# First MLP in six tiles of 512 tokens instead of eight of 384, with attention ending in the fourth tile

## The chip, the cores and the metric

The kernel runs on one core of a Trainium2 chip. The metric is the device time of one execution in microseconds (us), the median over several runs. Engines are named as in the profile: PE is the matrix engine (TensorE), PEld its weight loads, DVE the vector engine, ACT the scalar engine, POOL GpSimd, SP the engine whose queue issues nearly all DMAs here.

## The reference

Chunked attention feeds a first MLP, and that a second MLP, all in float32:

```python
# attention: q, k, v [4, 8, 768, 64], chunks of 32 queries; each sees 8 memory keys,
# 16 keys to the left, its own 32 and 8 to the right
scores = scale * np.matmul(q_c, k_full.transpose(0, 1, 3, 2))
scores = scores - np.max(scores, axis=-1, keepdims=True)
a = np.exp(scores)
a = a / (np.sum(a, axis=-1, keepdims=True) + 1e-09)
out[:, :, c_start:c_end] = np.matmul(a, v_full)
...
# first MLP: x [3072, 512], w_in [512, 2048], w_out [2048, 512]
h = x @ w_in
g = np.where(h > 0.0, h, alpha * (np.exp(np.minimum(h, 0.0)) - 1.0))
x = (g @ w_out).astype(np.float32)
# second MLP, same sizes
h = x @ w_in
r = np.maximum(h, 0.0)
g = s * (r * r) + b
return (g @ w_out).astype(np.float32)
```

## The kernel before

**Attention** works on 24 units of 128 tokens (four chunks, all heads). A unit goes through three steps: `step_S` (scores into a PSUM tile psS, then the softmax on DVE with its exponential on ACT, into `sm`), `step_P` (the transpose of `sm` into `pt`) and `step_V` (values into psV, then `to_x`). For the first `NU0` units (6) the steps are issued separately and `step_P` transposes on PE (psP, line 251) with a copy by ACT. From unit `NU0` on `step_P` uses 16 DVE stream transposes (line 258), and `step_VS` puts the values of one unit and the scores of the next behind each other on PE (psVS). The results of the first two tiles are split at once into a high and a low fp32r part (`xh`, `xl`); later ones go to DRAM (`x_dram`) and come back with `load_x`.

**First MLP.** Its tokens are cut into eight tiles of 384 (`sizes`), its hidden units into 16 blocks c of 128. A step (t, c) is `h1`: 12 matmuls of 128 x 128 weights against 384 columns into one PSUM bank psH (4 blocks of the contraction, three products each: high x high, high x low, low x high), then on ACT and DVE the activation `g` and its split into gh and gl; and, two steps behind, `out1`: 12 matmuls into four PSUM banks acc, three into each. I call 12 such matmuls a half-step and number the steps 0 to 127. The order of steps is written out: tile 0 with blocks 0 to 5, all of tile 1, the rest of tile 0 (its first part goes by way of `part_dram`), then tiles 2 to 7. So step 6 is (1, 0), step 22 is (0, 6), step 32 is (2, 0).

**Work beside the MLP steps.** `beside` mixes attention into the steps: units 0 to 2 come ahead of step 0, units 3 to 5 beside steps 0 to 5, none in tile 1, units 6 to 8 beside the rest of tile 0, the others evenly over tiles 2 to 4 (up to `TATT`). The weights of the first MLP arrive as int64 bits of doubles; `weights_to` turns them into fp32r pairs with work on ACT and DVE (`to_f32`, `split_w`), up to the end of tile 1. From `TATT` on `prepared` does the like for the second MLP's weights (`prepare`, with sums for a Strassen-like scheme) into `s_dram`, until `NFREE` blocks of the last tile are done. Then the buffers of the first `NFREE` blocks' weights (pool wpa) are given up and `load_blocks` fetches the second MLP's input.

**Second MLP.** Three tiles of 1024 tokens, seven products instead of eight blocks; every matmul there has 512 columns already (psH with `xc` moving, then psL with g2h and g2l moving).

The order within an engine is fixed when the program is built, by a scheduler that follows the order of the code with small shifts; each engine runs its instructions in that order. 16 KB of each partition are kept for descriptors of DMAs that GpSimd issues; the kernel issues none there.

Of the kernel before, what the change touches and what calls it, by code (L numbers as in the profile page):

```python
# [27 lines left out]
NP = H // 2  # L28
NU0 = 6
HF = 6  # L30
TATT = 5
NFREE = 8
MICRO = 8
# [20 lines left out]
def tile_attention_then_two_mlps(ctx, tc, q_in, k_in, v_in, w1, w2, s_in, b_in, out):  # L54
# [27 lines left out]

    sizes = [3] * 8
    assert sum(sizes) == NU
# [213 lines left out]
    def load_x(t):  # L298

        X[t] = xh, xl = x_tiles((t + 1) % 2)  # L300
        nc.sync.dma_start(out=f(xl), in_=x_dram[:, :, starts[t] * U:(starts[t] + sizes[t]) * U])
        nc.scalar.activation(out=xh, in_=f(xl), func=AF.Copy)
        sub(xl, f(xl), xh)
# [60 lines left out]
    def put_out(t, c, n):  # L364
# [6 lines left out]
        if c == NF - 1 or c == HF - 1 and split:  # L371
            for m, acc in enumerate(ACC[t]):
                with tc.high_priority(400):
                    if c == NF - 1 and split:
                        o = PART.pop(m)
                        nc.vector.tensor_tensor(out=o, in0=o, in1=acc[:, :n], op=ALU.add)
                    else:
                        o = big_tile(n, t >= TATT and m > 0 or m == 3 and t >= 2)
                        if m % 2:
                            nc.vector.tensor_copy(o, acc[:, :n])  # L380
                        else:
                            nc.scalar.activation(out=o, in_=acc[:, :n], func=AF.Copy)
                store = nc.scalar if t == NTILE1 - 1 else nc.sync
                store.dma_start(out=y_dram[:, m, t0:t0 + n] if c == NF - 1 else part_dram[:, m, :n], in_=o)
# [184 lines left out]
    def mlp1_step(t, c):  # L569
# [6 lines left out]
        elif t == 0:  # L576
            a0, total, k, ks = ready[1], ready[2] - ready[1], min(c - HF, NF - HF - 4), NF - HF - 3
        elif 1 < t < TATT:
            a0, total, k, ks = ready[2], len(steps) - ready[2], NF * (t - 2) + c, NF * (TATT - 2)

# [4 lines left out]
        elif t == 1:  # L585
            n0 = 8 * HF + 12
            wt = [(w1, max(n0 + (MICRO * NF - n0) * (2 * c + z) // 28, MICRO * (c + z)), 4) for z in (1, 2)]
        if c == 0 and t == TATT:
            actx.close()
# [24 lines left out]
    def prepared(t, n):  # L614

        want = min(NPREP * (2 * NF * (t - TATT) + n) // (2 * NF * (NTILE1 - TATT) - 2 * (NF - NFREE)), NPREP)
        while t >= TATT and p2["n"] < want:
            next(p2["steps"])
            p2["n"] += 1
# [182 lines left out]
```

## Time and profile before

| what | value |
|---|---|
| median of 3 runs | 1097.02 us (1095.85 to 1098.19) |
| the profiled execution: its own time | 1097.48 us |
| its span | 1095.7 us |
| PE busy in the span | 1076.3 us (98%) |
| DVE busy | 783.9 us (72%) |
| ACT busy | 591.9 us (54%) |
| mean granted PE clock | 0.992 of full speed |

Busy time of PE counts a matmul from its start to its modelled end, and matmuls overlap, so 98% does not say that the array works at its peak; the spacing of starts says how fast the stream runs. The span leaves out 1.78 us of the execution's own time.

### The profile page before, as it was taken

Reading aid. Unit: us, or ns where it says so; the run is one execution under the profiler, and the core shown is the slowest. Engines: PE = TensorE matmul, PEld = TensorE weight load, DVE = VectorE, ACT = ScalarE, POOL = GpSimd, SP = SyncE. Lnnn points to the kernel's source line nnn. Section 1 sums busy time; section 2 is a strip of 40 time slices with the busy share of each in tenths; the row PEclk is TensorE's granted clock in tenths of the full one; section 3 lists DMA queues with packets and bytes.
Section 4 is the critical chain, followed back from the end, with each engine's and each line's share of the span. In section 5 each row is a group of like instructions: output and inputs, shape, how many; then the busy total and the mean of one; then the engine's idle time right before and its main releaser. Section 6 shows DMA issues by size and latency. Waiting matters only on the chain.

```text
span 1095.7 us, 20629 instructions
## 1 busy us (share of the span) xinstructions
PE 1076.3 (98%) x8206; PEld 964.4 (88%) x8206; DVE 783.9 (72%) x1299; ACT 591.9 (54%) x939; POOL 0.7 (0%) x6
## 2 busy tenths in 40 slices
PE   7999999999999999999999999999999999999998
PEld 5889999999999999999999987788888788888886
DVE  6899856777777777898884656796266695375844
ACT  4888534344344346887875455644355653355542
POOL 0000000000000000000000000000000000000000
PEclk7999999999999999999999999999999999999999
DMA  8965032442433316888876366777767777776773
GB/s 305 377 223 214 1 109 94 146 144 93 142 117 121 114 40 206 328 329 303 328 289 253 90 192 190 240 211 224 229 192 196 222 207 226 207 193 192 205 190 124
DMA packets 98113, 213.70 MB, mean 195 GB/s; under 512 B 9952, under 2 KB 27360, under 8 KB 95968
## 3 DMA queue, kind: packets, MB, share of 16 engines
q1 hardware_dynamic: 97440, 211.59, 60.3%
q8 instruction: 65, 1.06, 0.4%
q10 hardware_dynamic: 576, 0.79, 0.2%
q14 instruction: 32, 0.26, 0.1%
HBM read 164.89 MB, written 47.45 MB: 194 GB/s over the span
## 4 chain that ended last, share of the span: by engine, by line
PE 87%; DVE 6%; DMA 4%; ACT 3%; issue 1%; SPq 0%; ACTq 0%; DVEq 0%
PE psH L326 14%; PE psH L328 14%; PE psH L327 14%; PE psL L327 7%; PE psL L328 7%; PE acc L326 7%; PE psL L326 7%; PE acc L327 7%; PE acc L328 7%; DVE pt L258 2%; DMA xc<-y_dram 1%; PE psVS L278 1%; DMA xl<-x_dram 1%; PE psVS L219 1%; PE psV L278 1%
## 5 line engine op out<-in xcount | busy, mean ns | idle before, releaser
L326 PE MATMUL psH<-xh,w 128*128 128x384 f32 x512 | 174.9, 342 | 2.4 <-ACT pt L180 1.0
L326 PE MATMUL acc<-gh,w 128*128 128x384 f32 x512 | 172.7, 338 | 1.3 <-DVE big L380 0.8
L328 PE MATMUL psH<-xh,w 128*128 128x384 f32 x512 | 173.0, 338 | 0.0
L327 PE MATMUL psH<-xl,w 128*128 128x384 f32 x512 | 172.6, 337 | 0.2 <-DVE xl L184 0.2
L328 PE MATMUL acc<-gh,w 128*128 128x384 f32 x512 | 171.8, 336 | 0.0
L327 PE MATMUL acc<-gl,w 128*128 128x384 f32 x512 | 171.7, 335 | 0.0
L702 ACT ACTIVATE g2h<-g 128x1024 fp32r<-128x1024 f32 x84 | 88.9, 1058 | 95.6 <-PE psL L328 95.5
L327 PE MATMUL psL<-g2l,ws 128*128 128x512 f32 x336 | 133.0, 396 | 1.4 <-DVE g2l L184 1.4
L184 DVE TENSOR_TENSOR g2l<-g,g2h 128x1024 fp32r<-128x1024 f32 x84 | 102.3, 1222 | 44.3 <-ACT g2h L702 44.0
L328 PE MATMUL psL<-g2h,ws 128*128 128x512 f32 x336 | 132.9, 395 | 0.0
L326 PE MATMUL psL<-g2h,ws 128*128 128x512 f32 x336 | 132.5, 396 | 0.1
L326 PE MATMUL psH<-xc,ws 128*128 128x512 f32 x336 | 131.7, 397 | 0.5 <-ACT p L653 0.5
L327 PE MATMUL psH<-xc,ws 128*128 128x512 f32 x336 | 131.0, 390 | 0.0
L328 PE MATMUL psH<-xc,ws 128*128 128x512 f32 x336 | 131.0, 390 | 0.0
L350 ACT ACTIVATE g<-psH 128x384 f32<-128x384 f32 x128 | 62.5, 488 | 111.9 <-PE psH L328 65.3
L180 ACT ACTIVATE gh<-g 128x384 fp32r<-128x384 f32 x128 | 67.0, 523 | 88.0 <-DVE g L352 86.9
L352 DVE SCALAR_TENSOR_TENSOR g<-g,psH 128x384 f32<-128x384 f32 x128 | 70.4, 550 | 47.8 <-ACT g L351 46.9
L326 PEld LDWEIGHTS psH<-xh,w 128*128 128x128 f32 x512 | 96.7, 189 | 5.1 <-ACT pt L180 1.2
L326 PEld LDWEIGHTS acc<-gh,w 128*128 128x128 f32 x512 | 96.1, 188 | 2.8 <-DVE big L380 1.1
L327 PEld LDWEIGHTS psH<-xl,w 128*128 128x128 f32 x512 | 96.7, 189 | 0.5 <-DVE xl L184 0.4
L328 PEld LDWEIGHTS psH<-xh,w 128*128 128x128 f32 x512 | 96.7, 189 | 0.2
L327 PEld LDWEIGHTS acc<-gl,w 128*128 128x128 f32 x512 | 96.2, 188 | 0.1
(97 smaller groups left out, 1667.9 us busy)
## 6 DMA issues: line engine op xcount, KB each, us to landing
ws<-s_dram SPq DMA_DIRECT2D x336, 256.0 KB, 3.0
raw<-w SPq DMA_DIRECT2D x64, 512.0 KB, 5.5
s_dram<-right SPq DMA_DIRECT2D x16, 1024.0 KB, 4.6
kb<-k SPq DMA_DIRECT2D x24, 512.0 KB, 5.5
v<-v SPq DMA_DIRECT2D x24, 512.0 KB, 4.1
s_dram<-left SPq DMA_DIRECT2D x16, 768.0 KB, 3.6
q<-q SPq DMA_DIRECT2D x24, 256.0 KB, 5.4
out<-r SPq DMA_DIRECT2D x24, 256.0 KB, 3.5
```

Source lines behind the costliest of these rows:

```text
L180: return nc.scalar.activation(out=hi, in_=src, func=AF.Copy)
L184: return nc.vector.tensor_tensor(out=lo, in0=src, in1=f(hi), op=ALU.subtract)
L219: mm = nc.tensor.matmul(ps[o, z, r * NCK:(r + 1) * NCK], q[rows, r * U + c * CH:r * U + (c + 1) * CH], kb[rows, r, c * NCK:(c + 1) * NCK], ...
L258: nc.vector.transpose(out=pt[k * CH:(k + 1) * CH, :, rows], in_=sm[rows, :, z, n0:n0 + CH])
L278: nc.tensor.matmul(ps[r % 2 * D:(r % 2 + 1) * D, z, o:o + CH], v[rows, (r * NC + c) * D:(r * NC + c + 1) * D], pt[rows, r, cs], start=True ...
L326: nc.tensor.matmul(o, sa(a[0]), sb(b[0]), start=first, stop=False, skip_group_check=again)
L327: nc.tensor.matmul(o, sa(a[0]), sb(b[1]), start=False, stop=False, skip_group_check=again)
L328: return nc.tensor.matmul(o, sa(a[1]), sb(b[0]), start=False, stop=last, skip_group_check=again)
L350: nc.scalar.activation(out=g[:, :n], in_=ps[:, :n], func=AF.Relu, scale=-1.0)
L352: nc.vector.scalar_tensor_tensor(out=g[:, :n], in0=g[:, :n], scalar=-1.0, in1=ps[:, :n], op0=ALU.add, op1=ALU.max)
L702: nc.scalar.activation(out=gh, in_=g[:, block], func=AF.Copy)
```

## The change

The first MLP gets six tiles of 512 tokens (four units each). Tile 0 now takes units 0 to 3 ahead of step 0, tile 1 units 4 to 7 beside steps 0 to 5, units 8 to 11 stand beside the rest of tile 0, and units 12 to 23 in tile 2 and the first eight steps of tile 3 (`ATT_END`). Separate attention steps with PE transposes go to eight units (`NU0`), the pool given up early holds ten blocks (`NFREE`), and preparation of the second MLP's weights runs from step (3, 8) to step (5, 10). The descriptor space shrinks from 16 KB to 1 KB to make room for the wider buffers. There are 96 steps now; step 22 is still (0, 6).

```diff
--- before.py
+++ after.py
@@ -26,10 +26,10 @@
 UPB = S // U
 NU = B * UPB
 NP = H // 2
-NU0 = 6
+NU0 = 8
 HF = 6
-TATT = 5
-NFREE = 8
+ATT_END = (3, 8)
+NFREE = 10
 MICRO = 8
 HN, NT2 = 512, 3
 ORDER = (1, 2, 6, 5, 7, 3, 4)
@@ -80,7 +80,7 @@
         n = turn[step, phase[0]] = turn.get((step, phase[0]), -1) + 1
         return names[n % len(names)]
 
-    sizes = [3] * 8
+    sizes = [4] * 6
     assert sum(sizes) == NU
     MAXN = max(sizes) * U
     starts = [sum(sizes[:i]) for i in range(len(sizes))]
@@ -297,7 +297,7 @@
 
     def load_x(t):
 
-        X[t] = xh, xl = x_tiles((t + 1) % 2)
+        xh, xl = X[t] = tuple(x[:, :, :sizes[t] * U] for x in x_tiles((t + 1) % 2))
         nc.sync.dma_start(out=f(xl), in_=x_dram[:, :, starts[t] * U:(starts[t] + sizes[t]) * U])
         nc.scalar.activation(out=xh, in_=f(xl), func=AF.Copy)
         sub(xl, f(xl), xh)
@@ -375,7 +375,7 @@
                         o = PART.pop(m)
                         nc.vector.tensor_tensor(out=o, in0=o, in1=acc[:, :n], op=ALU.add)
                     else:
-                        o = big_tile(n, t >= TATT and m > 0 or m == 3 and t >= 2)
+                        o = big_tile(n, len(op) > 1 and m > 0 or m == 3 and t >= 2)
                         if m % 2:
                             nc.vector.tensor_copy(o, acc[:, :n])
                         else:
@@ -575,8 +575,8 @@
             a0, total, k, ks = ready[0], ready[1] - ready[0], c, HF
         elif t == 0:
             a0, total, k, ks = ready[1], ready[2] - ready[1], min(c - HF, NF - HF - 4), NF - HF - 3
-        elif 1 < t < TATT:
-            a0, total, k, ks = ready[2], len(steps) - ready[2], NF * (t - 2) + c, NF * (TATT - 2)
+        elif t > 1 and (t, c) < ATT_END:
+            a0, total, k, ks = ready[2], len(steps) - ready[2], NF * (t - 2) + c, NF * (ATT_END[0] - 2) + ATT_END[1]
 
         wt = [(w1, 0, 4)] * 2
         if t == 0 and c < HF:
@@ -585,7 +585,7 @@
         elif t == 1:
             n0 = 8 * HF + 12
             wt = [(w1, max(n0 + (MICRO * NF - n0) * (2 * c + z) // 28, MICRO * (c + z)), 4) for z in (1, 2)]
-        if c == 0 and t == TATT:
+        if (t, c) == ATT_END:
             actx.close()
             op.append(mctx.enter_context(tc.tile_pool(name="op2", bufs=2)))
             p2["prep"] = early[1].enter_context(tc.tile_pool(name="prep", bufs=2, side="right", reuse_waits="tile"))
@@ -613,8 +613,9 @@
 
     def prepared(t, n):
 
-        want = min(NPREP * (2 * NF * (t - TATT) + n) // (2 * NF * (NTILE1 - TATT) - 2 * (NF - NFREE)), NPREP)
-        while t >= TATT and p2["n"] < want:
+        begin = 2 * (NF * ATT_END[0] + ATT_END[1])
+        want = min(NPREP * (2 * NF * t + n - begin) // (2 * NF * (NTILE1 - 1) + 2 * NFREE - begin), NPREP)
+        while (t, n) > (ATT_END[0], 2 * ATT_END[1]) and p2["n"] < want:
             next(p2["steps"])
             p2["n"] += 1
 
@@ -782,7 +783,7 @@
     import concourse.bacc as bacc
     from concourse.bass_utils import run_bass_kernel_spmd
 
-    nc = bacc.Bacc("TRN2", target_bir_lowering=False, num_devices=1)
+    nc = bacc.Bacc("TRN2", target_bir_lowering=False, num_devices=1, dynamic_dma_scratch_size=1024)
     q, k, v = pack(q, k, v, mem_k, mem_v)
     arrays = {
         "q": q,
```

How this moves instructions is shown at three places. Names end in buffer numbers where one operation has several.

First, PE around the first step of the first MLP (psP and psV are steps of attention, psS scores, sm_103 and sm_104 the two softmax buffers in turn, w_0 the weights of block 0). Before:

```order
L251 MATMUL psP<-ident,sm_103 128x128 x4
L278 MATMUL psV<-pt,v 64x32 x32
L219 MATMUL psS<-kb,q 32x64 x32
L326 MATMUL psH<-xh,w_0_382 128x384
L327 MATMUL psH<-xl,w_0_382 128x384
```

After, from the same row on:

```order
L251 MATMUL psP<-ident,sm_103 128x128 x4
L278 MATMUL psV<-pt,v 64x32 x32
L219 MATMUL psS<-kb,q 32x64 x32
L251 MATMUL psP<-ident,sm_104 128x128 x4
L278 MATMUL psV<-pt,v 64x32 x32
L219 MATMUL psS<-kb,q 32x64 x32
L326 MATMUL psH<-xh,w_0_433 128x512
L251 MATMUL psP<-ident,sm_103 128x128 x4
L327 MATMUL psH<-xl,w_0_433 128x512
```

One more unit (transposes of sm_104, values, scores) stands ahead of the first psH matmul, and the transposes of the unit behind it come after that first matmul instead of after the whole half-step.

Second, DVE in tile 1, from one activation g to the next (raw, t and w are the conversion of the weights, the number behind the name is the block). Before:

```order
L352 SCALAR_TENSOR_TENSOR g<-g,psH 128x384
L184 TENSOR_TENSOR w_7_1131<-t,w_7_1131 128x512
L138 SCALAR_TENSOR_TENSOR t<-raw_8_977,t 128x512
L184 TENSOR_TENSOR gl<-g,gh 128x384
L135 SCALAR_TENSOR_TENSOR t<-raw_8_1043 128x512
L135 SCALAR_TENSOR_TENSOR t<-raw_9_1081 128x512
L184 TENSOR_TENSOR w_8_1186<-t,w_8_1186 128x512
L138 SCALAR_TENSOR_TENSOR t<-raw_8_1043,t 128x512
L352 SCALAR_TENSOR_TENSOR g<-g,psH 128x384
```

After:

```order
L352 SCALAR_TENSOR_TENSOR g<-g,psH 128x512
L138 SCALAR_TENSOR_TENSOR t<-raw_8_1157,t 128x512
L135 SCALAR_TENSOR_TENSOR t<-raw_8_1223 128x512
L135 SCALAR_TENSOR_TENSOR t<-raw_9_1261 128x512
L380 COPY big<-acc_893 128x512
L184 TENSOR_TENSOR gl<-g,gh 128x512
L184 TENSOR_TENSOR w_8_1366<-t,w_8_1366 128x512
L138 SCALAR_TENSOR_TENSOR t<-raw_8_1223,t 128x512
L138 SCALAR_TENSOR_TENSOR t<-raw_9_1261,t 128x512
L352 SCALAR_TENSOR_TENSOR g<-g,psH 128x512
```

Both pieces run from the activation of step 7, (1, 1), to that of step 8. Six conversions and one gl stand between the two in either; after has a copy of an accumulator (big, acc) besides, which stood ahead of step 7 before, and g and gl have 512 columns.

Third, PE at the last attention unit (one psV, since no scores follow). Before:

```order
L328 MATMUL acc_4655<-gh,w_13_1597 128x384
L326 MATMUL acc_4656<-gh,w_13_1597 128x384
L327 MATMUL acc_4656<-gl,w_13_1597 128x384
L328 MATMUL acc_4656<-gh,w_13_1597 128x384
L278 MATMUL psV<-pt,v 64x32 x32
L326 MATMUL psH<-xh,w_0_382 128x384
L327 MATMUL psH<-xl,w_0_382 128x384
```

After:

```order
L328 MATMUL acc_4270<-gh,w_5_1136 128x512
L326 MATMUL acc_4271<-gh,w_5_1136 128x512
L327 MATMUL acc_4271<-gl,w_5_1136 128x512
L328 MATMUL acc_4271<-gh,w_5_1136 128x512
L278 MATMUL psV<-pt,v 64x32 x32
L326 MATMUL psH<-xh,w_8_1366 128x512
L327 MATMUL psH<-xl,w_8_1366 128x512
```

It stood behind the out1 of block 13 of tile 4, with block 0 of tile 5 next; it now stands behind block 5 and ahead of block 8 of tile 3.

## Rows read from the trace of the kernel before

**Rows 1.** The page's busy times: engine, busy us (share of the span), instructions

```profile
PE 1076.3 (98%) x8206; PEld 964.4 (88%) x8206; DVE 783.9 (72%) x1299; ACT 591.9 (54%) x939; POOL 0.7 (0%) x6
```

**Rows 2.** The page's granted PE clock in 40 slices of 27.4 us, tenths of full speed

```profile
PEclk7999999999999999999999999999999999999999
```

**Rows 3.** Stretches by stage: start:end length, busy us of each engine, PE clock, DMA, GB/s

```profile
0.00:28.30 28.30, 21.46 (x546) 16.67 (x546) 18.02 (x38) 12.22 (x20) 0.70 (x6) 0.78 0.84 308
28.30:76.20 47.90, 43.64 (x586) 38.48 (x578) 45.06 (x93) 41.80 (x81) 0.00 (x0) 0.95 0.77 294
76.20:136.60 60.40, 60.36 (x386) 58.99 (x387) 55.55 (x106) 43.83 (x86) 0.00 (x0) 1.00 0.35 130
136.60:182.90 46.30, 46.21 (x499) 45.34 (x498) 28.79 (x66) 18.60 (x35) 0.00 (x0) 1.00 0.37 116
182.90:416.80 233.90, 231.48 (x3010) 224.82 (x3008) 174.32 (x421) 96.04 (x182) 0.00 (x0) 1.00 0.34 110
416.80:550.30 133.50, 133.50 (x773) 133.50 (x770) 116.15 (x215) 105.90 (x197) 0.00 (x0) 1.00 0.85 307
550.30:621.10 70.80, 70.80 (x409) 70.80 (x408) 48.29 (x79) 42.38 (x78) 0.00 (x0) 1.00 0.57 210
621.10:1095.70 474.60, 468.88 (x2018) 375.79 (x2016) 297.69 (x284) 231.13 (x264) 0.00 (x0) 1.00 0.71 202
```

**Rows 4.** Stretches without attention, PE alone: 384 columns, psL, psH of the second MLP

```profile
470.00:600.00 130.00, 130.00 (x751) 1.00 0.83 305
1015.00:1090.00 75.00, 75.00 (x323) 1.00 0.63 179
807.00:821.50 14.50, 14.50 (x66) 1.00 0.70 195
```

**Rows 5.** Timeline of PE, second MLP, first and last psH of an unbroken run

```profile
806.68 0.39 PE L326 MATMUL psH<-xc,ws 128*128 128x512 f32 x1
...
821.41 0.39 PE L328 MATMUL psH<-xc,ws 128*128 128x512 f32 x1
```

**Rows 6.** Timeline of PE at the start: start us, length, operation [idle before]

```profile
22.79 1.11 PE L251 MATMUL psP<-ident,sm 128*128 128x128 f32 x4
...
24.65 1.72 PE L278 MATMUL psV<-pt,v 64*64 64x32 f32 x56 [0.75 <-ACT pt L180]
...
26.86 0.44 PE L278 MATMUL psV<-pt,v 64*64 64x32 f32 x8 [0.49 <-issue]
...
27.22 1.18 PE L219 MATMUL psS<-kb,q 64*32 64x64 f32 x64
...
28.34 0.69 PE L326 MATMUL psH<-xh,w 128*128 128x384 f32 x1
...
32.09 0.52 PE L328 MATMUL psH<-xh,w 128*128 128x384 f32 x1
...
32.41 0.82 PE L251 MATMUL psP<-ident,sm 128*128 128x128 f32 x4
```

**Rows 7.** Timeline of DVE: softmax end of unit 3, activations g of steps 0 and 6

```profile
29.98 0.68 DVE L237 TENSOR_TENSOR sm<-sm,rs 128x512 f32<-128x512 f32 x1
...
33.73 0.55 DVE L352 SCALAR_TENSOR_TENSOR g<-g,psH 128x384 f32<-128x384 f32 x1 [1.87 <-ACT g L351]
...
75.64 0.55 DVE L352 SCALAR_TENSOR_TENSOR g<-g,psH 128x384 f32<-128x384 f32 x1
```

**Rows 8.** Timeline of PE, last acc and first psH around one psVS step

```profile
239.72 0.34 PE L328 MATMUL acc<-gh,w 128*128 128x384 f32 x1
...
241.84 0.44 PE L326 MATMUL psH<-xh,w 128*128 128x384 f32 x1
```

**Rows 9.** Groups by line, DVE: count, busy us, mean ns, idle before

```profile
L352 DVE SCALAR_TENSOR_TENSOR g<-g,psH 128x384 f32<-128x384 f32 x128 | 70.4, 550 | 47.8 <-ACT g L351 46.9
...
L138 DVE SCALAR_TENSOR_TENSOR t<-raw,t 128x512 int32<-128x512 int32 x64 | 43.8, 686 | 0.4
...
L258 DVE STREAM_TRANSPOSE pt<-sm 32x128 f32<-32x128 f32 x288 | 87.1, 303 | 5.8
```

## Prediction, made before the changed kernel ran

> **What bounds the kernel now.** I read the busy times first: PE is taken for 98% of the span, DVE for 72%, ACT for 54% [rows 1]. That is a mean over unlike stages, so next I cut the span where the order of steps changes [rows 3]; the eight lengths add up to 1095.7 us. The reader should see two kinds of stage. From 76.2 us on PE is busy almost without a gap in every stage (231.48 of 233.9 us in the stretch with most of the attention, all of 133.5 and 70.8 us behind it): there the time is the number of matmuls by the spacing of their starts, plus what attention puts between them. Ahead of 76.2 us it isn't so. PE is busy for 21.46 of the first 28.3 us and its clock is 0.78; from 28.3 to 76.2 us DVE is busy for 45.06 of 47.9 us, so it sets the pace there. The second MLP (621.1 to the end, 474.6 us) has neither new instructions nor another order, and I take it as it is.
>
> The spacing comes from stretches without attention [rows 4]. A window counts every matmul that touches it, so I add one matmul's length to the window: (130 + 0.34)/751 = 173.6 ns for 384 columns. At 2.4 GHz, the upper of the two clock levels, 384 columns take 160 ns, so 13.6 ns are extra. For 512 columns (213.3 ns) the second MLP gives two answers: psL (75 + 0.40)/323 = 233.4 ns, and psH 14.73 us between the first and last start of 66 matmuls, 226.6 ns [rows 4, 5]. The clock stands at full in all three.
>
> **Term 1, the matmuls of the first MLP.** Before: 8 x 16 x 24 = 3072 at 173.6 ns = 533.3 us. After: 6 x 16 x 24 = 2304 of 512 columns. The trace has none of these, so I bound them by the two rows: at 226.6 ns 522.1 us (-11.2), at 233.4 ns 537.8 us (+4.5). What separates the rows isn't visible in the trace. By structure half of the new matmuls are like each: h1 takes high and low parts of one long-lived input and adds many products into one bank, as psH does; out1 takes parts that ACT and DVE have just written and changes the bank every three, as psL does. So I take the mean, 230.0 ns: 529.9 us, **-3.4 us**, and keep both ends for the range.
>
> The spacing has an extra of 13.3 to 20 ns for each matmul [rows 4, 5]. The Trainium skill, "TensorE: Matmul & The Clock Gate", section Back-to-back issue gap, gives columns/2.4 plus 2.5 ns for an isolated warm matmul; by that the term would be 3072 x 162.5 = 499.2 against 2304 x 215.8 = 497.3 us, an estimate of -1.9 us. The trace doesn't agree with its size.
>
> **Term 2, the start, up to step 22.** Before, 136.6 us [rows 3]. Of these 42 half-steps (22 h1, 20 out1) of 12 x 173.6 ns = 2.083 us are 87.5 us, so 49.1 us are other things. After, step by step:
> - The first psH waits for unit 3. Its softmax is done at 29.98 + 0.68 = 30.7 us [rows 7], and nothing ahead of that has moved on DVE. Transposes 1.11, the copy to `pt` 0.75 (the idle ahead of psV), values some 2.1 (24.65 to 27.22 without the 0.49 idle), scores 1.12 (27.22 to 28.34) [rows 6]: first psH at 35.7 us, not 28.3.
> - The first half-step runs at the lower level, 1.2 GHz: 3.75 us for 11 starts [rows 2, 6], 0.32 us each once running. I take 0.427 us for 512 columns, 5.1 us, and 1.1 us for the transposes that now lie inside: until 41.9 us. Activation g of step 0 then comes 9.3 us later than before, at 43.0 us.
> - From g of step 0 to g of step 6 DVE needed 41.9 us (33.73 to 75.64) [rows 7], nearly all busy. By the two orders that stretch has six weight conversions and a copy fewer, three softmax operations, one split and two small ones more, so about three full-size ones fewer at some 0.6 us each (0.686 us with their overlap [rows 9]), and twelve g and gl of 512 columns, 0.13 us longer each (686 ns against 550). That is 42.2 us: no change. DVE would release step 8 at about 85 us.
> - PE needs more in that stretch now: 13 half-steps of 12 x 230.0 ns = 2.76 us are 35.9 us, and four units (transposes 0.8, values and scores 1.95 as in the psVS step between 239.72 + 0.17 and 241.84 [rows 6, 8]) 11.0 us. From 41.9 that makes 88.8 us; with 1 us for waits between two engines that are both nearly full, step 8 starts at 89.8 where it started at 76.2.
> - From there to step 22 28 half-steps: 77.3 us, and 1.5 us of waits (2.1 before: 60.4 - 58.3). Conversions go on: the nine DVE instructions from one g to the next are 5.4 us at 0.6 each for a step of 5.52 us, where eight with two narrow ones were 4.6 us for 4.17.
>
> So step 22 starts at 168.6 us. 42 x 2.76 = 115.9 us of that are matmuls, 52.7 us are other things: **+3.6 us**, for two units more. Bounds: 0 if the later start keeps PE at its upper clock level and nothing waits, +8 if DVE and PE hold each other up as they did for 8.6 us between 28.3 and 76.2 us (47.9 less 14 half-steps, three units and the slow clock's 1.9).
>
> **Term 3, attention from step 22 on.** Before, 136.6 to 416.8 us is 280.2 us for 58 steps of 4.17 us (241.6 us) [rows 3]: 38.6 us more, for 17 psVS steps of 1.95 us [rows 8], one psV of about 1.1 us and 4.3 us of waits. After, 15 psVS steps: 29.3 + 1.1 + 3.8 us of waits in proportion = 34.2 us, **-4.4 us**. They stand closer, two steps (11.0 us) and 1.95 us apart, where DVE needs 16 x 0.303 us for the transposes, some 3 us for the softmax and 2.8 us for two steps' g and gl: 10.6 of 13 us. That is the cover; if DVE came late, each unit would make PE wait, with 0.5 us each +7.5 us.
>
> **At no cost**, because PE's own work covers them: preparation of the second MLP's weights (116.15 us of DVE in 133.5 us, and PE never idle [rows 3]) gets 34 wider steps, 188 us, for 40 of 167 us; fewer and wider activations on ACT and DVE; the copies of acc, with a half-step of 2.76 us ahead of the next use instead of 2.08; the second MLP's first blocks, which start four steps (22 us) ahead of the end instead of six (25 us). If these blocks came late, the end of the 70.8 us stretch would show up to 3 us. `load_x` moves 1 MB instead of 0.75, but the units that fill a tile now end four steps ahead of it. The 1 KB left to GpSimd's descriptors costs nothing, since GpSimd issues no DMA.
>
> **Sum.** -3.4 + 3.6 - 4.4 = -4.2 us: span 1091.5 us. The profiled execution took 1.78 us more than its span, and the median of the runs lies 0.46 us below it, so I add 1.3 us: **1092.8 us**.
>
> **Rivals.**
> - *All new matmuls at psH's spacing.* The extra per matmul would be a constant 13.3 ns, which fits 384 columns and psH; psL speaks against it. Term 1 is -11.2, the rest as above less 0.5 in term 2: span 1083.2, time 1084.5 us.
> - *All at psL's spacing, the side of slower.* For it: gh and gl are written and used just as g2h and g2l are, and 4/3 of 173.6 is 231.5 already. Against it: 384 columns show no such part. Term 1 is +4.5, term 2 +4: span 1099.8, time 1101.1 us. It turns at 231.8 ns: from there on the wider tile loses on matmuls and start what attention gives.
> - *The units don't become cheaper.* DVE in the denser attention is late by 0.5 us for each: +7.5, 1100.3 us. The busy sum of 10.6 in 13 us speaks against it, the chain from scores by softmax and transposes to values, all on one queue, for it.
> - *The start doesn't cost.* Term 2 at its lower bound: 1089.2 us.
>
> **How the numbers follow.** I give the forecast 0.38 with 1089 to 1097 us for itself (the last rival, 0.04, falls in it), psH's spacing throughout 0.28, psL's 0.22, late units 0.08. The range from 1084 to 1102 us takes in both bounds of the matmuls and leaves out the far ends of term 2 on either side, some 2 in 10. A measurement of this kernel tells 0.2% from no change, 2.2 us: faster is below 1094.8 us, slower above 1099.2 us. Faster: all of psH's case, some 0.26 of the forecast's 0.42 with the cheap start, and 0.03 of the rest: 0.57. Slower: most of psL's case and of the late units, 0.22. Within: 0.21.
>
> **What would show it.** Windows without attention give the spacing of 512-column matmuls directly, psH and acc apart: between 226.6 and 233.4 ns, one at each if my reading of the structure holds. The first psH should start at 35 to 36 us, step 8 near 90 and step 22 near 169 us. Between step 22 and the last psV PE should idle no more than 4 us, and behind it not at all until the second MLP, which should take 474 to 475 us. I am wrong if one spacing holds for both halves, if PE waits for pt in most units, or if step 8 starts beyond 93 us.

## The result

The changed kernel takes 1106.25 us (median of 5 runs, 1102.97 to 1107.67) against 1097.02 us before: a ratio of 1.0082, 95% interval 1.0059 to 1.0106. It is slower by some 9 us. The profiled execution has a span of 1105.4 us, 9.7 us more than before.

The page's busy times and the granted PE clock (slices of 27.6 us), to be read beside [rows 1, 2]:

```profile
PE 1081.8 (98%) x7446; PEld 869.7 (79%) x7446; DVE 768.3 (70%) x1199; ACT 576.8 (52%) x839; POOL 0.7 (0%) x6
...
PEclk7899999998999899999999999999999999999999
```

The shares say nothing: DVE and ACT have less to do than before, PE is taken for 98% again. The clock line does: besides the second digit, at the start, its tenth and fourteenth, 249 to 276 and 359 to 387 us, are 8 where [rows 2] have 9 from the second slice on.

Stretches by stage of the changed kernel: start:end length, busy us of PE, PEld, DVE, ACT and POOL, PE clock, DMA, GB/s. The cuts are the first psH, step 8, step 22, step 32, the step behind the last unit, step 64 and the second MLP:

```profile
0.00:34.80 34.80, 25.22 (x678) 19.86 (x678) 24.76 (x52) 16.32 (x27) 0.70 (x6) 0.73 0.87 325
34.80:85.40 50.60, 50.13 (x641) 39.14 (x634) 48.58 (x96) 44.73 (x82) 0.00 (x0) 0.99 0.83 308
85.40:163.80 78.40, 77.91 (x338) 63.03 (x337) 50.17 (x82) 47.19 (x83) 0.00 (x0) 1.00 0.20 64
163.80:231.50 67.70, 65.53 (x753) 52.80 (x752) 49.55 (x112) 25.56 (x41) 0.00 (x0) 1.00 0.43 137
231.50:404.70 173.20, 167.65 (x2049) 134.10 (x2047) 130.11 (x302) 62.07 (x99) 0.00 (x0) 0.95 0.35 115
404.70:448.90 44.20, 44.20 (x199) 36.19 (x194) 35.38 (x62) 33.08 (x57) 0.00 (x0) 1.00 0.77 272
448.90:631.60 182.70, 182.70 (x793) 148.68 (x792) 131.92 (x213) 117.31 (x193) 0.00 (x0) 1.00 0.66 239
631.60:1105.40 473.80, 468.49 (x2017) 375.95 (x2016) 297.86 (x284) 230.54 (x264) 0.00 (x0) 1.00 0.69 203
```

The reader should see that one stretch is unlike the others: from 231.5 to 404.7 us PE is idle for 5.55 us and has a clock of 0.95, which over 173.2 us is another 8.7 us of work lost. Before, the two stretches with units had 2.51 us of idle time in all and a clock of 1.00 [rows 3]. With the 2.17 us idle from 163.8 to 231.5 us, 7.7 us are idle here.

How long the matmuls take is read from first psH to first psH of neighbouring steps in a stretch without units. Timeline of PE, steps 4 and 5, then 13 and 14 of the fifth tile:

```profile
471.12 0.40 PE L326 MATMUL psH<-xh,w 128*128 128x512 f32 x1
...
476.72 0.40 PE L326 MATMUL psH<-xh,w 128*128 128x512 f32 x1
...
521.22 0.39 PE L326 MATMUL psH<-xh,w 128*128 128x512 f32 x1
...
526.66 0.39 PE L326 MATMUL psH<-xh,w 128*128 128x512 f32 x1
```

Each pair is 24 matmuls, 12 psH and 12 acc: 5.60 us (233.3 ns each) at step 4, 5.44 us (226.7 ns) at step 13. Steps 0 to 9 of a tile, whose weights lie in the pool `wpa`, have the first spacing, steps 10 to 15 with weights in `wpb` the second, h1 and out1 alike. That makes 60 x 5.60 + 36 x 5.44 = 531.8 us.

So the 9.7 us by stage, against [rows 3] and with 531.8 and 533.3 us of matmuls taken out where they lie: matmuls -1.5; other work up to step 22 47.0 us for 49.1, -2.1; other work from step 22 to the end of the first MLP 52.8 us for 38.6, **+14.2**; second MLP 473.8 us for 474.6, -0.8. The sum is +9.8.

What PE waits for from 163.8 to 404.7 us (the chain of waits of PE: who waits, for what, us in all, times, longest):

```profile
PE psVS L278 <- DVE pt L258: 5.6, 16, 1.1
PE acc L326 <- DVE big L376: 1.8, 1, 1.8
PE psV L278 <- DVE pt L258: 0.3, 1, 0.3
```

PE waits for `pt` inside seven of the fifteen psVS steps. And behind the long waits the clock falls. PE alone around three of them (the first window stands behind the 1.8 us for `acc`, over at 253.9 us): start:end length, busy us (instructions), clock, DMA, GB/s:

```profile
256.00:260.00 4.00, 4.00 (x130) 0.50 0.13 14
312.00:316.00 4.00, 1.96 (x52) 1.00 0.00 0
316.00:320.00 4.00, 4.00 (x100) 0.57 0.53 143
372.00:376.40 4.40, 3.35 (x124) 0.74 0.00 0
376.40:380.00 3.60, 3.60 (x16) 0.50 0.66 220
```

PE stands for 2.04 of 4 us behind 312 us, and in the next 4 us its clock is 0.57, near the lower level of 1.2 GHz. At 376.4 us it waits for nothing, and still runs at half the clock. Not every wait has this behind it: the 2.17 us idle from 163.8 to 231.5 us left the clock at 1.00. Of the +14.2 us, 5.2 are more idle time and 8.7 the clock; 15 units in place of 17 (with the last psV 30.4 us for 34.3) take 3.9 off. The last 4 us lie inside the units that wait: their matmuls come in small groups there, each counted as busy to its modelled end, so idle time shows only a part of the wait (step 24 is 1.4 us too long with 0.70 us of idle time).

### The profile page after: what moved, and what is told of

It reads as the page before. It is cut to its first block, busy times and chain, and to the rows that moved or that the text cites. A ratio compares the mean times of both kernels' runs of the same rounds, so it can differ in the third digit from the quotient of the medians.

```text
span 1105.4 us, 18800 instructions
## 1 busy us (share of the span) xinstructions
PE 1081.8 (98%) x7446; PEld 869.7 (79%) x7446; DVE 768.3 (70%) x1199; ACT 576.8 (52%) x839; POOL 0.7 (0%) x6
## 4 chain that ended last, share of the span: by engine, by line
PE 80%; DVE 10%; DMA 5%; ACT 3%; issue 1%; SPq 0%; DVEq 0%; ACTq 0%
PE psH L326 13%; PE psH L328 13%; PE psH L327 12%; PE psL L327 7%; PE psL L328 7%; PE psL L326 7%; PE acc L326 6%; PE acc L327 6%; PE acc L328 6%; DVE pt L258 3%; DMA xc<-y_dram 1%; PE psVS L278 1%; DMA xl<-x_dram 1%; DMA x_dram<-xs 1%; DVE gl L184 1%
## 5 line engine op out<-in xcount | busy, mean ns | idle before, releaser
L326 PE MATMUL acc<-gh,w 128*128 128x512 f32 x384 | 153.2, 399 | 2.3 <-DVE big L376 1.8
L326 PE MATMUL psH<-xh,w 128*128 128x512 f32 x384 | 153.6, 400 | 0.2 <-DVE g L352 0.2
L327 PE MATMUL psH<-xl,w 128*128 128x512 f32 x384 | 152.1, 396 | 0.0
L328 PE MATMUL psH<-xh,w 128*128 128x512 f32 x384 | 152.0, 396 | 0.0
L327 PE MATMUL acc<-gl,w 128*128 128x512 f32 x384 | 151.8, 395 | 0.0
L328 PE MATMUL acc<-gh,w 128*128 128x512 f32 x384 | 151.7, 395 | 0.0
L327 PE MATMUL psL<-g2l,ws 128*128 128x512 f32 x336 | 133.0, 396 | 0.4 <-DVE g2l L184 0.4
L326 PE MATMUL psH<-xc,ws 128*128 128x512 f32 x336 | 131.6, 396 | 1.1 <-ACT p L654 1.1
L326 PE MATMUL psL<-g2h,ws 128*128 128x512 f32 x336 | 132.2, 396 | 0.0
L327 PE MATMUL psH<-xc,ws 128*128 128x512 f32 x336 | 130.9, 390 | 0.0
L350 ACT ACTIVATE g<-psH 128x512 f32<-128x512 f32 x96 | 57.1, 595 | 122.1 <-PE psH L328 109.9
L352 DVE SCALAR_TENSOR_TENSOR g<-g,psH 128x512 f32<-128x512 f32 x96 | 65.8, 685 | 77.3 <-ACT g L351 76.7
L180 ACT ACTIVATE gh<-g 128x512 fp32r<-128x512 f32 x96 | 60.5, 631 | 77.5 <-DVE g L352 76.9
L326 PEld LDWEIGHTS acc<-gh,w 128*128 128x128 f32 x384 | 72.6, 189 | 20.0 <-DVE big L376 2.3
L326 PEld LDWEIGHTS psH<-xh,w 128*128 128x128 f32 x384 | 72.7, 189 | 17.7 <-DVE g L352 0.6
L328 PEld LDWEIGHTS psH<-xh,w 128*128 128x128 f32 x384 | 72.7, 189 | 16.9 <-DVE w L184 0.2
L327 PEld LDWEIGHTS psH<-xl,w 128*128 128x128 f32 x384 | 72.7, 189 | 16.6 <-DVE xl L184 0.3
L328 PEld LDWEIGHTS acc<-gh,w 128*128 128x128 f32 x384 | 72.5, 189 | 16.6
```

The lines of the kernel that those rows point to most:

```text
L180: return nc.scalar.activation(out=hi, in_=src, func=AF.Copy)
L326: nc.tensor.matmul(o, sa(a[0]), sb(b[0]), start=first, stop=False, skip_group_check=again)
L327: nc.tensor.matmul(o, sa(a[0]), sb(b[1]), start=False, stop=False, skip_group_check=again)
L328: return nc.tensor.matmul(o, sa(a[1]), sb(b[0]), start=False, stop=last, skip_group_check=again)
L350: nc.scalar.activation(out=g[:, :n], in_=ps[:, :n], func=AF.Relu, scale=-1.0)
L352: nc.vector.scalar_tensor_tensor(out=g[:, :n], in0=g[:, :n], scalar=-1.0, in1=ps[:, :n], op0=ALU.add, op1=ALU.max)
```

## The experiments

A unit is one psVS step here, its interval the steps between two units plus 1.95 us. The wait of a step is its length less 24 matmuls and the unit's 1.95 us, a slow clock included. Idle is PE's idle time from step 22 to the step behind the last unit, lost clock the length of a stretch by what its clock lacks to 1.00, both in us and from windows as above (the clock has two digits, so this one is good to about 1 us). The ratio is to the kernel before on the same chip. That kernel took 1097.6 to 1098.8 us in the median on the chips of the experiments, so a difference of two medians below can be off by 1 to 2 us where the chips differ, and the ratios are the safer measure.

| run | median us | ratio, 95% interval | idle | lost clock |
|---|---|---|---|---|
| before | 1097.02 | | 2.5 | 0 |
| changed kernel | 1106.25 | 1.0082 (1.0059-1.0106) | 7.7 | 8.7 |
| e1_pad | 1095.26 | 0.9984 (0.9968-0.9999) | 8.2 | 5.1 |
| e2_before_pad | 1090.57 | 0.9929 (0.9910-0.9949) | | |
| e10_pad96 | 1099.66 | 1.0020 (1.0002-1.0038) | | |
| e3_att_3_14 | 1095.54 | 0.9973 (0.9963-0.9982) | 3.4 | 2.0 |
| e4_half_transposes | 1092.15 | 0.9947 (0.9927-0.9968) | 1.1 | 0 |
| e5_before_tatt4 | 1135.35 | 1.0336 (1.0313-1.0359) | 11.1 | 12.3 |
| e11_load_later | 1105.63 | 1.0067 (1.0044-1.0090) | 6.6 | 4.7 |
| e13_no_sums | 1103.20 | 1.0040 (1.0025-1.0055) | 8.4 | 5.1 |
| e14_copy_behind | 1100.68 | 1.0027 (1.0011-1.0044) | 4.5 | 2.0 |
| e7_pad_3_14 | 1085.50 | 0.9887 (0.9865-0.9909) | 4.6 | 0 |
| e8_pad_4_0 | 1085.52 | 0.9884 (0.9864-0.9905) | 3.1 | 0 |
| e9_pad_3_14_late8 | 1082.66 | 0.9862 (0.9841-0.9882) | 4.6 | 2.0 |
| e12_pad_3_14_nu12 | 1078.75 | 0.9829 (0.9812-0.9846) | 1.9 | 0 |
| e15_best_copy_behind | 1077.37 | 0.9813 (0.9794-0.9832) | 2.2 | 0 |

### The spacing of the matmuls

In the program's memory plan the left-side tiles (xh, xl, gh, gl, g2h, g2l, `wpb`) start 64 bytes past a multiple of 128, the right-side ones (`wpa`, ws, xc) 96 bytes past one. The pairs that start alike (x or g with `wpb`, xc with ws) are those at 226.7 ns, the others (x or g with `wpa`, g2h or g2l with ws) those at 233.3; neither the input's place nor the weight's alone sorts them. One small tile moves the whole left side:

```diff
     b_sb = const.tile([P, 1], F32, name="b_sb")
+    pad = const.tile([P, 1], F32, name="pad")
```

**e1_pad**, in the changed kernel.

> The changed kernel with an unused tile of 4 bytes a partition ahead of all others on the left side of SBUF, which moves the start of every left-side tile by 32 bytes (inputs xh, xl, gh, gl, g2h, g2l and the later weights wpb), while the tiles on the right side (the early weights wpa, pieces ws, blocks xc) stay. Nothing is computed differently. Theory A (the spacing of 512-column matmuls depends on whether the two operands start at the same place within 128 bytes): all operands then start alike, so the 60 steps with weights of wpa go from 5.60 to 5.44 us (-9.6 us) and the 1008 psL of the second MLP from 233.4 to 226.7 ns (-6.7 us): about 16 us faster than the changed kernel, 1090 us. Theory B (the spacing follows how the operands were written and used, as the prediction took it): no spacing changes, 1106 us. Theory C (it follows the age or the pool of the weights): no spacing changes either.

Timeline of PE in this run (the added line moves L326 to L327), first psH of steps 4 and 5 of the fifth tile:

```profile
466.42 0.39 PE L327 MATMUL psH<-xh,w 128*128 128x512 f32 x1
...
471.86 0.39 PE L327 MATMUL psH<-xh,w 128*128 128x512 f32 x1
```

5.44 us: every step of the first MLP is now at 226.7 ns. For psL, PE's windows from 1000 to 1070 us of the changed kernel, of e1_pad, of e2_before_pad and of e10_pad96:

```profile
1000.00:1070.00 70.00, 70.00 (x303) 1.00 0.70 196
```
```profile
1000.00:1070.00 70.00, 70.00 (x309) 1.00 0.72 202
```
```profile
1000.00:1070.00 70.00, 70.00 (x309) 1.00 0.72 207
```
```profile
1000.00:1070.00 70.00, 70.00 (x306) 1.00 0.72 198
```

With one matmul's length added, (70 + 0.40)/303 is 232.3 ns, /309 227.8 and /306 230.1; the means from start to start are 233.4, 226.7 and 229.0 ns. Theory A holds, B and C fall: nothing was computed differently. The time fell by 11 us and not 16, since step 22 starts no sooner in the profiled execution (164.3 us: the first psH came at 35.94 us, 1.1 us later than in the changed kernel, and step 8 1.6 us later, of which the faster steps had won back 1.1 us by step 22), and the waits did not shrink: faster steps bring the units closer together.

**e2_before_pad**, the same line in the kernel before.

> The kernel before with the unused tile that moves all left-side tiles by 32 bytes; nothing else is changed. Theory A (the spacing of 512-column matmuls depends on whether the two operands start at the same place within 128 bytes, at 384 columns it doesn't): psL goes from 233.3 to 226.7 ns, 1008 x 6.7 ns = -6.7 us, the first MLP stays at 173.3 ns a matmul: 1090 to 1092 us. Theory B (the spacing follows how operands are written): no change, 1097 to 1098 us. If the first MLP were moved as well, more than 10 us would be gained.

7.0 us were won, psL moved, and the steps of 384 columns stayed at 4.16 us: the kernel before could have had this too, and at 384 columns there is nothing to gain.

**e10_pad96**, `[P, 24]` in place of `[P, 1]`.

> The changed kernel with an unused tile of 96 bytes a partition in place of 4: left-side tiles then start 64 bytes away from those of the right side within 128 bytes, and at the same place within 64 bytes. Theory A64 (what counts is the place within 64 bytes): steps with weights of wpa and psL stay at 226.7 ns a matmul, as in the run with 4 bytes, 1094 to 1097 us. Theory A128 (the place within 128 bytes): both are back at 233.3 ns as in the changed kernel, 1105 to 1108 us.

Neither: steps of early weights took 5.49 us (228.9 ns), psL 229.0 ns, and the steps with weights of `wpb`, whose start is moved together with the inputs', stayed at 5.44 us. With operands 64 bytes apart a third of the cost is left. That the relative start counts is shown; what in the chip looks at it isn't.

### The waits of the denser attention

**e3_att_3_14**:

```diff
-ATT_END = (3, 8)
+ATT_END = (3, 14)
```

> The changed kernel with attention ending six steps later, at step 14 of the fourth tile: twelve units in 30 steps of tiles 2 and 3 in place of 24, that is 2.5 steps and 1.95 us (15.6 us) for a unit in place of 2 steps (13.0 us). Theory A (the chain on DVE and ACT from the scores to the last transpose fills the 13 us, so that whatever is queued ahead of it, the sums of the first tile with its stored part or the split of the next tile's input, makes PE wait for pt): 2.6 us of slack for a unit, the waits of tiles 2 and 3 fall from about 18 to 5 us or less, those of the four units in steps 22 to 28 (4.5 us) stay: -12 to -15 us against the changed kernel, some 1092 us. Theory B (the waits come from transfers that end late and not from the density): the long steps at 35, 43 and 51 stay, not more than 5 us are won, some 1102 us. Preparation of the second MLP has 28 steps in place of 34; if it doesn't fit, PE waits behind the last unit and the gain is smaller.

PE alone, its two stretches with units:

```profile
165.90:233.70 67.80, 66.35 (x754) 0.97 0.43 137
233.70:426.50 192.80, 190.89 (x2194) 1.00 0.32 104
```

The waits did as theory A said: the idle time fell by 4.3 us, the lost clock by 6.7. The time fell by 10.7 us, somewhat less than the 12 to 15 given (by the two ratios it is 12 us). Steps 43 and 51 are no longer long, step 35 still waits 1.9 us, and steps 24 to 28, whose density is the same, 4.7 us as in the changed kernel.

**e4_half_transposes**:

```diff
-        for c in range(NC):
+        for c in range(NC // 2):
             rows = slice(c * CH, (c + 1) * CH)
```

> The changed kernel with 8 of the 16 transposes of each unit from unit 8 on left out (the later half of pt keeps old values, so this part of the attention is not computed): DVE's chain from scores to values is 2.4 us shorter, PE's work and all transfers are the same. Theory A (the length of the chain makes PE wait): waits of attention from step 22 on fall from 22.4 to about 6 us, what is left at steps 35 and 43, and the half clock behind the waits goes with them: -14 to -18 us, some 1090 us. Theory B (late transfers): the long steps stay as they are, -3 us at the most.

```profile
163.70:227.10 63.40, 63.40 (x754) 1.00 0.45 146
227.10:385.90 158.80, 157.73 (x2050) 1.00 0.38 126
```

PE's windows: 1.07 us idle, the clock never falls, -14.1 us. With the same order of units, the same transfers and the same work on PE, 2.4 us less in DVE's chain take the waits away, but for 2.0 us at step 35. DVE has less to do in all here, so this run alone doesn't tell the chain from the busy time.

**e5_before_tatt4**, the density alone, in the kernel before:

```diff
-TATT = 5
+TATT = 4
```

> The kernel before with attention ending one tile earlier (tiles of 384, eight of them): 15 units in 32 steps of 4.17 us in place of 48, 2.13 steps and 1.95 us, 10.8 us for a unit. Nothing else of the change is made. Theory A (the chain of one unit, some 11.3 us with the g and gl that are queued inside it, and the 1.95 us of its matmuls, is the least interval of two units, about 13.2 us): each unit makes PE wait some 2.4 us, 25 to 40 us in all, 1122 to 1137 us. Theory B (what counts is DVE's busy time, 9.9 us of the 10.8): nearly no waits, 1097 to 1102 us.

```profile
137.70:184.40 46.70, 46.38 (x497) 1.00 0.36 115
184.40:389.10 204.70, 193.94 (x2649) 0.94 0.38 122
```

PE's windows again: 10.76 us idle behind 184.4 us, clock 0.94. 36.7 us slower, in theory A's range; by DVE's busy time it would have been 5 at most, and DVE, for which PE waits, is busy for only 157.44 of the 204.7 us. The interval of two units has a floor: the chain on DVE and ACT plus the unit's own matmuls, and the steps' g and gl stand in the same queues.

The chain can be read in the changed kernel itself. Timeline around a unit that waits hardly at all, the one whose values come in step 49: its scores on PE, then DVE's first and third softmax operation, each behind a wait for ACT, and its last transposes:

```profile
346.42 0.86 PE L219 MATMUL psVS<-kb,q 64*32 64x64 f32 x64
...
347.95 0.69 DVE L231 TENSOR_REDUCE nmx<-psVS 128x8 f32<-128x512 f32 x1 [0.49 <-ACT xs L180]
...
350.06 0.69 DVE L234 TENSOR_REDUCE sums<-sm 128x8 f32<-128x512 f32 x1 [0.70 <-ACT sm L233]
...
354.45 3.88 DVE L258 STREAM_TRANSPOSE pt<-sm 32x128 f32<-32x128 f32 x12
```

From the end of the scores (347.28 us) to the end of the transposes (358.33 us) are 11.05 us, and with the 1.95 us of values and scores that is the whole interval of 13.0 us. Over the fifteen units the same stretch takes 10.5 to 15.2 us, 12.1 in the median: nothing is left over for anything else in these queues.

### What makes single units late

The waits are uneven: seven of fifteen units wait hardly at all, the one of step 43 waits 4.5 us. Timeline of the changed kernel around it, three engines put in order of time (start, length, operation, count, idle before with its releaser):

```profile
297.12 0.63 ACT L180 ACTIVATE gh<-g 128x512 fp32r<-128x512 f32 x1 [2.56 <-DVE g L352]
...
298.83 1.91 ACT L302 ACTIVATE xh<-xl 128x2048 fp32r<-128x2048 f32 x1 [1.09 <-DMA xl<-x_dram]
...
300.65 0.58 ACT L350 ACTIVATE g<-psH 128x512 f32<-128x512 f32 x1
...
300.77 2.29 DVE L184 TENSOR_TENSOR xl<-xl,xh 128x2048 fp32r<-128x2048 f32 x1 [1.30 <-ACT xh L302]
...
303.58 0.69 DVE L228 TENSOR_TENSOR sm<-psVS,cmask 128x512 f32<-128x512 f32 x1
...
313.65 1.93 DVE L258 STREAM_TRANSPOSE pt<-sm 32x128 f32<-32x128 f32 x6
...
314.33 0.31 PE L278 MATMUL psVS<-pt,v 64*64 64x32 f32 x6 [1.08 <-DVE pt L258]
...
316.56 1.18 PE L219 MATMUL psVS<-kb,q 64*32 64x64 f32 x64
```

The reload of the next tile's input (`load_x`) has its transfer still under way when ACT comes to its copy; DVE waits for that copy, and the softmax stands behind both. Three runs look at this.

**e11_load_later**:

```diff
-        if c == NF - 4 and 1 <= (t or 1) < NTILE1 - 1 and t != 1:
+        if c == NF - (3 if t else 4) and 1 <= (t or 1) < NTILE1 - 1 and t != 1:
```

> The changed kernel with the input of tiles 3 and later loaded and split one step later (behind step 13 of the tile ahead, not step 12). Theory A (the copy of 2048 columns on ACT, its wait for the transfer and the subtraction on DVE stand in the queue ahead of the softmax of the unit of step 43, and cost it its slack): the wait of 4.5 us at step 43 falls below 1 us, and comes up at step 45 or is hidden in the step without a unit; the time stays within 4 us of the changed kernel. Rival (the wait has another cause, the masked unit or the unit's own place): step 43 stays at 11.9 us.

Inconclusive. Step 43 stayed at 11.57 us, but the edit did not move the copy: the scheduler that orders the queues put it at the same place (297.71 us).

**e13_no_sums**, without `sub(xl, f(xl), xh)` and without the sum with `PART`:

```diff
         nc.scalar.activation(out=xh, in_=f(xl), func=AF.Copy)
-        sub(xl, f(xl), xh)
...
-                        o = PART.pop(m)
-                        nc.vector.tensor_tensor(out=o, in0=o, in1=acc[:, :n], op=ALU.add)
```

> The changed kernel without two pieces of work: the subtraction that splits the reloaded input of a tile (DVE, 2.29 us, and its wait for the copy on ACT) and the sum of the first tile's stored part (four loads, four additions on DVE that become two copies each on ACT and DVE). The output is then not the sum that is asked for. Theory A (these pieces stand in DVE's queue between the scores and the softmax of one unit each): the wait of 6.1 us at step 35 falls below 3 us, that of 4.5 us at step 43 below 1 us, the wait at step 51 stays; 1096 to 1100 us. Rival (density alone, any unit may be hit): the waits turn up at other steps and their sum stays above 18 us, 1103 us or more.

Theory A fell as it was put: step 35 still waited 5.1 us, step 43 5.6 us, and the time, 1103.20 us, is just the rival's, though the steps that wait are the same. Timeline of this run, ACT and DVE (lines behind L302 have a number one lower):

```profile
301.66 1.92 ACT L302 ACTIVATE xh<-xl 128x2048 fp32r<-128x2048 f32 x1 [2.63 <-DMA xl<-x_dram]
...
304.75 0.69 DVE L351 SCALAR_TENSOR_TENSOR g<-g,psH 128x512 f32<-128x512 f32 x1 [4.00 <-ACT g L350]
```

DVE's 2.29 us are gone, and DVE stands 4.00 us instead: ACT waits 2.63 us for the transfer, copies for 1.92 us, and only then makes the g that DVE needs. The copy on ACT holds both engines.

**e14_copy_behind**, where `last_vs` holds the last matmul of the scores of each psVS step:

```diff
-        nc.scalar.activation(out=xh, in_=f(xl), func=AF.Copy)
+        copy = nc.scalar.activation(out=xh, in_=f(xl), func=AF.Copy)
+        if last_vs:
+            wait(copy, last_vs[-1])
```

> The changed kernel with one wait more: ACT's copy of a tile's reloaded input comes behind the scores of the unit that was issued last, so it can't stand in ACT's queue ahead of the activation g of two steps earlier while its transfer is under way. Nothing else is changed. Theory A2 (the wait of 4.5 us at step 43 comes from this copy, which waits for its transfer ahead of g, so that DVE's g and the softmax behind it come late): step 43 falls from 11.9 to 8.5 us or less, and the copy, whose transfer has then landed, costs the next unit 2 us or less; time 2 to 5 us below the changed kernel, 1101 to 1104 us. Rival (density alone, some unit in this stretch is hit whatever stands in the queue): the sum of the waits stays at 18 us or more, 1105 to 1107 us.

```profile
300.04 0.68 DVE L228 TENSOR_TENSOR sm<-psVS,cmask 128x512 f32<-128x512 f32 x1
...
313.52 1.91 ACT L302 ACTIVATE xh<-xl 128x2048 fp32r<-128x2048 f32 x1
...
315.71 2.28 DVE L184 TENSOR_TENSOR xl<-xl,xh 128x2048 fp32r<-128x2048 f32 x1
```

Timeline of this run: the copy now starts with no wait, 15 us later, and the mask of step 43's unit is no longer behind it. Step 43 takes 8.82 us in place of 11.93, and no step behind it took its wait over. The long step 51 went with it: in the changed kernel the copy for the next tile stood ahead of that unit's softmax in the same way (DVE's subtraction behind it at 360.88, the softmax only at 363.69 us, for scores that had ended at 360.40):

```profile
358.93 1.91 ACT L302 ACTIVATE xh<-xl 128x2048 fp32r<-128x2048 f32 x1 [1.32 <-DMA xl<-x_dram]
```

Here this copy comes at 381.89 us, and step 51 takes 7.54 us in place of 10.41, step 52, which held the half clock behind it, 5.70 in place of 7.71. This part of the waits was a transfer, by way of two queues. Of the 5.6 us won (8.6 between the profiled spans) not all need be the copies': step 35 is shorter too, 10.87 us, as it was in e11 (10.85 us). It was not taken apart further: in the changed kernel it holds DVE's sums of the first tile, for which the 1.8 us of `acc` above wait, and in e13 a copy that waits for a store.

### Versions with both causes treated

**e7_pad_3_14** has the small tile and `ATT_END = (3, 14)`.

> The changed kernel with both edits: the unused tile of 4 bytes and the end of attention at step 14 of the fourth tile. Theory A (spacing and density are two separate causes): the two gains against the changed kernel, 11.0 and 10.7 us, nearly add up, less 1 to 2 us since steps of 5.44 us leave a unit 0.4 us less slack than steps of 5.60 us: 1085 to 1087 us. Rival (both gains are the same time, so that faster matmuls only turn into waits for pt): 1094 us.

**e8_pad_4_0** has `ATT_END = (4, 0)`.

> As the run with both edits, but with the end of attention at the start of the fifth tile: 2.67 steps and 1.95 us, 16.5 us for a unit in tiles 2 and 3. Theory A: what is left of the waits in these tiles (3 to 4 us with 30 steps) goes too, 1083 to 1085 us. Rival: preparation of the second MLP has 26 steps, some 141 us, for 84 us of its own on DVE and 36 us of g and gl; if that is too tight, PE waits behind the last unit and the run is no faster than the one with 30 steps.

Spacing and density are two causes: their gains add up. Ending later still wins nothing more, as the rival said: the waits fall by 1.5 us, and behind the last unit PE is idle for 2.8 of 183.8 us.

**e9_pad_3_14_late8** spreads units 8 to 11 over eight steps:

```diff
-            a0, total, k, ks = ready[1], ready[2] - ready[1], min(c - HF, NF - HF - 4), NF - HF - 3
+            a0, total, k, ks = ready[1], ready[2] - ready[1], min(c - HF, NF - HF - 3), NF - HF - 2
...
-        if c == NF - 4 and 1 <= (t or 1) < NTILE1 - 1 and t != 1:
+        if c == NF - (4 if t else 3) and 1 <= (t or 1) < NTILE1 - 1 and t != 1:
```

> As the run with both edits, and units 8 to 11 are spread over eight steps of the first tile's end in place of seven (the input of the third tile is loaded one step later): two steps and 1.95 us, 12.8 us, for a unit where it was 1.75 steps, 11.5 us. Theory A (a unit needs some 13 us): the waits of 4.2 us at steps 24 to 28 fall to 2 us or less, 1083 to 1085 us. Rival: the later load meets the last sums of the first tile, and step 35 loses what is won.

The time can't be told from e7's (the intervals overlap), and the trace does not bear theory A out: steps 24 to 28 still wait over 4 us in all, step 24 more than in e7, steps 26 and 28 less.

**e12_pad_3_14_nu12** is e7 with `NU0 = 12`.

> The version with both edits (unused tile of 4 bytes, end of attention at step 14 of the fourth tile), and units 8 to 11 are transposed on PE as the first eight are (scores, transposes and values as steps of their own) in place of 16 transposes on DVE. Theory A: their chain is some 4.5 us shorter on DVE, the waits of 4.4 us at steps 24 to 28 go, and PE takes some 0.8 us more for each unit, 3.2 us: between -2 and +1 us against the version with both edits, 1083 to 1086 us. Rival: the transposes need a bank that psH also uses, and PE waits for it: 2 us or more slower, 1088 us.

6.8 us less than e7 (3.4 by the profiled spans), more than theory A gave: no idle time is left from step 22 to step 32, which took 64.7 us for 66.9 though PE transposes four units more, and the second MLP starts at 609.4 us for 612.4. **e15_best_copy_behind** adds e14's wait.

> The fastest version so far (unused tile of 4 bytes, end of attention at step 14 of the fourth tile, twelve units transposed on PE) with the same wait for ACT's copy. Theory A2: with 2.5 steps for a unit the copy is mostly covered already; at step 56 1.1 us are left to win: 1077 to 1079 us. Rival: the copy behind the scores meets the next softmax and costs it up to 2 us: 1080 to 1081 us.

1077.37 us: 1.9% below the kernel before, the fastest here; from e12 it can't be told apart. Step 56 no longer waits, step 35 waits 3.1 us.

## Why the prediction was wrong

**The step that failed is term 3**, attention from step 22 on: 52.8 us for the 34.2 foretold. The span lies 13.9 us above the 1091.5 of the sum; term 3 is +18.6 of that, term 1 +1.9, term 2 -5.7, the second MLP -0.8. Term 3 took the waits "in proportion", 3.8 us. Its cover was a sum of busy times, 10.6 of 13 us, which holds (DVE is busy for 130.11 of 173.2 us) and was the wrong thing to ask. A unit's softmax and transposes are one chain over two queues, not one, with ACT's exp in the middle and the steps' g and gl in between. That the length of this chain decides is shown by e5, where it sets the pace while DVE is busy for 77%, by e4, where it is shorter, and by its own 11.05 us above. It stood in the trace of before, at an interval that hid it. Timeline of one unit there, scores on PE and last transposes on DVE:

```profile
370.98 0.86 PE L219 MATMUL psVS<-kb,q 64*32 64x64 f32 x64
...
380.49 2.58 DVE L258 STREAM_TRANSPOSE pt<-sm 32x128 f32<-32x128 f32 x8
```

These are 11.2 us from the end of the scores (371.84 us) to the end of the transposes (383.07 us), and 13.2 us with the unit's own 1.95 us: no slack at all in the 13.0 us that term 3 foresaw. The rival "the units don't become cheaper" named it, with 0.5 us each and a chance of 0.08. That price was too low for two reasons that the runs show: a chain without slack passes on what stands ahead of it (the copies cost 3.1 us at step 43 and, with the half clock behind, 4.9 us at steps 51 and 52, e14), and the clock behind the longer waits costs as much again as the idle time (8.7 us beside 7.7; e4 gives both back, e3 most of both). No term had the clock in it.

**Term 1** was off by 1.9 us, by a reason that was wrong: 531.8 us for 529.9, inside its bounds. "What separates the rows isn't visible in the trace", and so I guessed at structure. The test that I named decided against me: h1 and out1 have one spacing within a step, and it changes with the weights' pool. e1 and e2 show that the relative start of the operands separates the two rows; h1 like psH and out1 like psL came from where xc, g2h and ws happened to lie. The pool borders stood in the kernel: 10 of 16 blocks at 233.3 and 6 at 226.7 ns would have given 230.8. That half of the matmuls at either spacing gave 230.0 was luck. By the Trainium skill, "TensorE: Matmul & The Clock Gate", section Back-to-back issue gap, the term was an estimate of -1.9 us, and -1.5 us were measured; but the page's 215.8 ns for an isolated matmul are not what the trace shows (226.7 to 233.3 ns), so this nearness is chance too.

**Term 2** had the wrong sign, -2.1 us for +3.6, which is below its lower bound of 0. The first psH came at 34.85 us (35.7), step 8 at 85.4 (89.8), step 22 at 163.8 (168.6). From step 8 on the 78.4 us agree with 78.8. Ahead of it DVE's 85 us held, and PE's 88.8 us were too much. Timeline of PE, step 0:

```profile
34.85 0.80 PE L326 MATMUL psH<-xh,w 128*128 128x512 f32 x1
...
36.70 0.40 PE L326 MATMUL psH<-xh,w 128*128 128x512 f32 x1
...
38.56 0.40 PE L328 MATMUL psH<-xh,w 128*128 128x512 f32 x1
...
39.96 0.50 PE L326 MATMUL psH<-xh,w 128*128 128x512 f32 x1
```

The eight starts behind 36.70 us are 0.232 us apart, at full clock; I had 0.427 us for the whole half-step, from the slow one of before [rows 6]. Step 0 took 5.11 us with its transposes and its values inside, where 6.2 stood for the half-step and its transposes alone.

**What held**: nothing waits from 404.7 us to the second MLP, though preparation began with 34 steps left, and the second MLP took 473.8 us.

## What to carry to other kernels

Before work is packed closer, compare the interval of its repeats with the length of its longest chain over all queues, not with each engine's busy share. Where no slack is left, as here, look for every copy in those queues that may wait for a transfer; 2.6 us more for each unit (e3) took most of the waits away. Price a wait of PE by itself and by the stretch at half clock that may follow it. When two groups of like matmuls have two spacings, look where their operands start in a partition before any other reason.

## What the runs showed of the hardware

For fp32r matmuls of 128x512 the spacing of starts was 226.7 ns with both operands starting at the same place within 128 bytes, 229.0 ns 64 bytes apart and 233.3 ns 32 bytes apart; at 384 columns 173.3 ns with or without the shift. One unused tile of 4 bytes was worth 7 us in the kernel before and 11 us in the changed one. And a unit that made PE stand for 2.04 of 4 us was followed by 4 us at a clock of 0.57 with no wait in them, while units that didn't wait left the clock at 1.00, and so did the waits of steps 24 to 28, 2.17 us of idle time in three units.
